# Attention with a gated feed-forward block on one core: a smaller first weight piece and short dummies at the start, the last block finished bank by bank at the end

## The chip, the core and the metric

The kernel runs on one core of a Trainium2 chip. The metric is the device time of one execution in microseconds (us). A profiled execution has a trace; its span is about 1.3 us shorter than the device time of the same execution (1284.5 against 1285.8).

Engines: TensorE (PE in the profile; its weight loads are PEld), VectorE (DVE), ScalarE (ACT), GpSimd (POOL), SyncE (SP, which here only issues transfers). PSUM is the memory, in banks, that TensorE's results land in. A dummy is a matmul whose result nobody reads; it stands at the start, where TensorE would otherwise be idle.

## The reference

```python
xn = layernorm(x)                                   # x: 2048 x 512
q  = (xn @ wq) in 32 heads of 128
o  = softmax(q k^T / sqrt(128)) v                   # k, v: 2048 cached rows a head
s  = o @ wo
h  = relu(xn @ W_gate) * (xn @ W_up)                # 512 -> 1792, 14 column blocks of 128
g  = silu(h @ W_down)
out = x + s * g
```

## The kernel before

It starts with the feed-forward block, one row block of 512 rows at a time, and the layernorm of the later row blocks is woven into the first one. The first row block ("the head") is not normalised before its matmuls: its four row tiles are only centred (the row scale is put in later), so that TensorE can start early. (Shortened.)

```python
FCS = [0, min(3, FC), min(8, FC), FC]        # weight pieces, in column blocks
load_x0(sp, 0); load_x0(act, 1)              # x row tiles 0 and 1
load_w(sp, Wg, 0); load_w(act, Wu, 0)        # first piece of both weights
load_x0(sp, 2); load_x0(act, 3)
load_w(sp, Wg, 1); load_w(sp, Wu, 1)
load_xq(1)                                   # x row tiles 4 to 7
load_w(sp, Wg, 2); load_w(sp, Wu, 2)
for Q in range(2, QB): load_xq(Q)            # x row tiles 8 to 11, 12 to 15
...
def head_ln():                               # after ten dummies of 512 columns
    ctok = {0: head_transpose(0, head_center(0))}
    warm_mm(2)                               # two more
    for n in range(4):
        ... head_tile(n, 0); head_transpose(n + 1); head_tile(n, 1); head_tile(n, 2)
```

Column blocks 0 to 2 of the head occupy the three slots of a ring of two PSUM banks each. Block 3 therefore waits for slot 0 (`ring_acquire`), until ScalarE's ReLU and VectorE's multiply of block 0 have read it. VectorE runs in program order, and between the multiplies of the first row block stand the layernorm statistics of later rows:

```python
def finish_gate_up(Q, fc, s, gtok, gu_tok):
    ... act.activation(gr_sb, gate bank, Relu)
    ... dve.tensor_tensor(hT[:, fc, :], gr_sb, up bank, mult)
    ring_tok[s] = [rtok, h_tok]
    if Q == 0: ln_task(fc)                   # statistics of row tile 4 + fc; every 4th: more
```

So the statistics of row tile 8 (`ln_task(4)`) come before the multiply of column block 5. At the end, the last attention block is normalised in two halves after all its score-times-value matmuls, then transposed on TensorE; then come the final output tiles 8 to 15 (output projection on TensorE; a multiply by g and an add of x on VectorE).

The softmax here doesn't subtract the row's maximum and nothing guards it: scores larger than these inputs give would overflow.

## Time and profile before

| | before |
|---|---|
| device time, median of 3 | 1286.27 us (1286.20 to 1286.35) |
| profiled execution | 1285.8 us, span 1284.5 us |
| busy share | TensorE 99%, ScalarE 78%, VectorE 30% |
| head's first gate tile | 6.32 us |
| second row block's first matmul | 44.02 us |
| last multiply of the output tiles | 1281.19 us |

The page of the profile says who is the bottleneck:

```profile
span 1284.5 us, 26708 instructions
...
PE 1266.6 (99%) x11813; PEld 835.2 (65%) x12040; DVE 380.5 (30%) x685; ACT 1001.7 (78%) x1109; POOL 13.2 (1%) x25
```

With TensorE at 99% only the two ends have room. The timeline of TensorE at the front (start, duration, engine, source line, operation, output and inputs, count; in brackets the idle time before and what ended it):

```profile
1.19 3.81 PE L369 MATMUL ps_r<-warm 128*128 128x512 bf16 x10 [1.19 <-DVE warm L234]
5.26 0.38 PE L359 MATMUL ps_acc<-ident,xc_sb 128*128 128x128 bf16 x4 [0.26 <-DVE xc_sb L349]
5.48 0.59 PE L369 MATMUL ps_r<-warm 128*128 128x512 bf16 x2
6.32 0.40 PE L397 MATMUL ps_r<-xcT,Wg_sb 128*128 128x128 bf16 x4 [0.24 <-ACT xcT L364]
...
13.15 0.81 PE L483 MATMUL ps_r<-xcT,Wg_sb 128*128 128x512 bf16 x3 [0.63 <-ACT gr_sb L449]
...
44.02 1.03 PE L483 MATMUL ps_r<-xnT,Wg_sb 128*128 128x512 bf16 x4
```

The line at 13.15 is block 3 waiting for its slot (one of its four matmuls is missing from the records; its first weight load is at 12.91):

```profile
12.91 0.56 PEld L483 LDWEIGHTS ps_r<-xcT,Wg_sb 128*128 128x128 bf16 x4 [0.56 <-ACT gr_sb L449]
```

The line at 44.02 is the first matmul of the second row block. From there to the end of the span it is 1240.5 us, so this start sums up everything that the front has won or lost.

VectorE at the end (L782 multiplies an output tile by g, L798 adds x, L688 and L691 normalise):

```profile
1271.02 0.69 DVE L782 TENSOR_TENSOR fin_tmp<-ps_r,g_sb 128x512 bf16<-128x512 f32 x1 [3.31 <-PE ps_r L774]
...
1273.59 0.17 DVE L688 RECIPROCAL rz_sb<-ps_acc 128x2 f32<-128x2 f32 x1 [0.60 <-PE ps_acc L737]
...
1274.33 0.42 DVE L691 TENSOR_TENSOR Onorm<-ps_acc,rz_sb 128x256 bf16<-128x256 f32 x1
1274.67 0.68 DVE L782 TENSOR_TENSOR fin_tmp<-ps_r,g_sb 128x512 bf16<-128x512 f32 x1
...
1275.60 0.68 DVE L782 TENSOR_TENSOR fin_tmp<-ps_r,g_sb 128x512 bf16<-128x512 f32 x1
...
1281.19 0.69 DVE L782 TENSOR_TENSOR fin_tmp<-ps_r,g_sb 128x512 bf16<-128x512 f32 x1
1281.79 0.75 DVE L798 TENSOR_TENSOR x_sb<-x_sb,fin_tmp 128x512 bf16<-128x512 bf16 x2
```

From 1274.67 on the multiplies follow each other every 0.93 us without idle time: VectorE, not TensorE, is the chain there.

### The profile page before, as it was taken

Reading aid. Unit: us, or ns where it says so; the run is one execution under the profiler, and the core shown is the slowest. Engines: PE = TensorE matmul, PEld = TensorE weight load, DVE = VectorE, ACT = ScalarE, POOL = GpSimd, SP = SyncE. Lnnn points to the kernel's source line nnn. Section 1 sums busy time; section 2 is a strip of 40 time slices with the busy share of each in tenths; the row PEclk is TensorE's granted clock in tenths of the full one; section 3 lists DMA queues with packets and bytes.
Section 4 is the critical chain, followed back from the end, with each engine's and each line's share of the span. In section 5 each row is a group of like instructions: output and inputs, shape, how many; then the busy total and the mean of one; then the engine's idle time right before and its main releaser. Section 6 shows DMA issues by size and latency. Waiting matters only on the chain.

```text
span 1284.5 us, 26708 instructions
## 1 busy us (share of the span) xinstructions
PE 1266.6 (99%) x11813; PEld 835.2 (65%) x12040; DVE 380.5 (30%) x685; ACT 1001.7 (78%) x1109; POOL 13.2 (1%) x25
## 2 busy tenths in 40 slices
PE   9999999999999999999999999999999999999998
PEld 5444466676666666666666666666666666666665
DVE  6433311112222222222222222222222222224355
ACT  3322399998888888888888888888888888888884
POOL 2100000000000000000000000000000000000000
PEclk9999999999999999999999999999999999999999
DMA  9600123232222332332221322323323322332202
GB/s 263 131 1 1 22 47 55 60 56 37 36 54 46 71 54 50 55 70 51 54 45 32 67 46 54 55 67 55 55 51 70 54 36 38 51 67 55 49 15 75
DMA packets 240977, 72.13 MB, mean 56 GB/s; under 512 B 227808, under 2 KB 240864, under 8 KB 240864
## 3 DMA queue, kind: packets, MB, share of 16 engines
q1 hardware_dynamic: 240048, 69.76, 28.5%
q8 instruction: 96, 1.57, 0.5%
q10 hardware_dynamic: 816, 0.66, 0.2%
q14 instruction: 17, 0.14, 0.0%
HBM read 32.77 MB, written 2.10 MB: 27 GB/s over the span
## 4 chain that ended last, share of the span: by engine, by line
PE 85%; ACT 12%; issue 1%; DVE 1%; DMA 0%; DVEq 0%
PE ps_acc L737 32%; PE ps_r L640 25%; ACT PT L650 12%; PE ps_r L573 9%; PE ps_r L594 8%; PE ps_acc L506 4%; PE ps_r L487 4%; PE ps_r L483 4%; PE ps_r L774 1%; DVE fin_tmp L782 0%; PE ps_r L397 0%; DMA x_sb<-in_A_x_dram 0%; DVE x_sb L798 0%; ACT gr_sb L449 0%; PE ps_acc L359 0%
## 5 line engine op out<-in xcount | busy, mean ns | idle before, releaser
L650 ACT ACTIVATE PT<-ps_r 128x1024 bf16<-128x1024 f32 x1024 | 952.5, 1054 | 167.7 <-PE ps_r L640 164.9
L737 PE MATMUL ps_acc<-V_sb,PT 128*128 128x129 bf16 x8192 | 776.5, 220 | 10.7
L737 PEld LDWEIGHTS ps_acc<-V_sb,PT 128*128 128x128 bf16 x8192 | 621.1, 98 | 241.7 <-ACT PT L650 3.5
L640 PE MATMUL ps_r<-QT_sb,KT_sb 128*128 128x512 bf16 x1837 | 675.1, 379 | 0.3
L667 DVE RECIPROCAL rz_sb<-ps_acc 128x4 f32<-128x4 f32 x127 | 23.3, 183 | 729.8 <-PE ps_acc L737 729.8
L640 PEld LDWEIGHTS ps_r<-QT_sb,KT_sb 128*128 128x128 bf16 x2048 | 195.0, 98 | 1.1 <-DVE QT_sb L584 0.4
L573 PE MATMUL ps_r<-xnT,Wq_sb 128*128 128x512 bf16 x511 | 130.9, 379 | 0.1
L594 PE MATMUL ps_r<-Wo_sb,OT_store 128*128 128x512 bf16 x447 | 114.4, 379 | 0.1
L584 DVE CAST QT_sb<-ps_r 128x512 bf16<-128x512 f32 x128 | 88.5, 692 | 48.1 <-PE ps_r L573 48.1
L573 PEld LDWEIGHTS ps_r<-xnT,Wq_sb 128*128 128x128 bf16 x512 | 49.9, 97 | 60.6 <-ACT PT L650 27.1
L670 DVE TENSOR_TENSOR Onorm<-ps_acc,rz_sb 128x512 bf16<-128x512 f32 x127 | 87.8, 691 | 4.4
L594 PEld LDWEIGHTS ps_r<-Wo_sb,OT_store 128*128 128x128 bf16 x448 | 43.8, 98 | 52.9 <-ACT PT L650 0.2
L449 ACT ACTIVATE gr_sb<-ps_r 128x512 bf16<-128x512 f32 x56 | 32.9, 595 | 49.6 <-PE ps_r L483 49.1
L607 DVE TENSOR_TENSOR s_acc<-s_acc,ps_r 128x512 f32<-128x512 f32 x96 | 66.0, 687 | 17.4 <-PE ps_r L594 17.4
L455 DVE TENSOR_TENSOR hT<-gr_sb,ps_r 128x512 bf16<-128x512 bf16 x56 | 38.4, 685 | 46.8 <-PE ps_r L487 42.2
L506 PE MATMUL ps_acc<-Wd_sb,hT 128*128 128x512 bf16 x220 | 48.8, 379 | 0.2
L487 PE MATMUL ps_r<-xnT,Wu_sb 128*128 128x512 bf16 x164 | 42.7, 379 | 0.2
L483 PE MATMUL ps_r<-xnT,Wg_sb 128*128 128x512 bf16 x165 | 42.6, 379 | 0.2
L506 PEld LDWEIGHTS ps_acc<-Wd_sb,hT 128*128 128x128 bf16 x224 | 21.9, 98 | 26.4
L514 ACT ACTIVATE sig_sb<-ps_acc 128x512 f32<-128x512 f32 x12 | 7.2, 597 | 29.5 <-PE ps_acc L506 29.5
L487 PEld LDWEIGHTS ps_r<-xnT,Wu_sb 128*128 128x128 bf16 x168 | 16.4, 98 | 19.8
L483 PEld LDWEIGHTS ps_r<-xnT,Wg_sb 128*128 128x128 bf16 x168 | 16.4, 98 | 19.8
(50 smaller groups left out, 181.0 us busy)
## 6 DMA issues: line engine op xcount, KB each, us to landing
V_sb<-in_A_v_cache_dram SPq DMA_DIRECT2D x32, 512.0 KB, 4.8
Wq_sb<-in_A_wq_dram SPq DMA_DIRECT2D x32, 128.0 KB, 2.5
Wo_sb<-in_A_wo_dram SPq DMA_DIRECT2D x8, 512.0 KB, 4.9
OT_store<-Onorm SPq DMA_TRANSPOSE x127, 2.4
Wd_sb<-in_B_W_down_dram SPq DMA_DIRECT2D x1, 1792.0 KB, 14.6
x_sb<-in_A_x_dram SPq DMA_DIRECT2D x3, 512.0 KB, 12.1
out_dram<-x_sb SPq DMA_DIRECT2D x6, 256.0 KB, 2.2
Wg_sb<-in_B_W_gate_dram SPq DMA_DIRECT2D x1, 768.0 KB, 10.3
```

Of the source, the lines that this page charges most:

```text
L455: dve.tensor_tensor(hT[par][:, fc, :], gr_sb[gk][:], ps_r[:, gb + 1, :], ALU.mult)
L483: ins = pe.matmul(ps_r[:, gb, :], Wg_sb[:, c, fs], xT[:, c, xs], start=(c == 0), stop=(c == DC - 1))
L487: ins = pe.matmul(ps_r[:, gb + 1, :], Wu_sb[:, c, fs], xT[:, c, xs], start=(c == 0), stop=(c == DC - 1))
L506: ins = pe.matmul(ps_acc[:, jb, 0:D], hT[par][:, fc, j * 128:(j + 1) * 128], Wd_sb[:, fc, :], start=(fc == 0), stop=(fc == FC - 1))
L573: ins = pe.matmul(ps_r[:, bank, :], Wq_sb[b][:, c, :], xnT[:, c, qs], start=(c == 0), stop=(c == DC - 1))
L584: etok = sem_qpe.sig(dve.tensor_copy(QT_sb[b][:, qs], ps_r[:, bank, :]))
L594: ins = pe.matmul(ps_r[:, bank, 0:D], OT_store[g % 2][:, hh, n * 128:(n + 1) * 128], Wo_sb[g % 2][:, hh, :], start=(hh == 0), stop=(hh == ...
L607: dve.tensor_tensor(s_acc[:, n, :], s_acc[:, n, :], ps_r[:, bank, 0:D], ALU.add)
L640: ins = pe.matmul(ps_r[:, 2 * s + tt, :], KT_sb[h % 2][:, t * 128:(t + 1) * 128], QT_sb[h % 2][:, qs], start=True, stop=True)
L650: act.activation(PT[pb][:], ps_r[:, 2 * s:2 * s + 2, :], ACTF.Exp, scale=scale)
L670: dve.tensor_tensor(Onorm[ob][:], o_ap, rz_sb[:].to_broadcast([128, 4, Dh]), ALU.mult))
L737: ins = pe.matmul(o_ap, PT[pb][:, tt, j * 128:(j + 1) * 128], V_sb[vb][:, t, 0:VW], start=(t == 0 and j % 2 == 0), stop=(t == KT - 1 and j ...
```

## The change

Its intent at the front: the first weight piece is smaller, so that it lands sooner; the dummies, which are meant to bring TensorE's clock up, are shorter and need no tile cleared by VectorE; block 3 uses the two accumulator banks, which are idle then. At the end: tiles 8 and 9 go ahead of the last score-times-value matmuls, these are done bank by bank, and ScalarE normalises the first bank. The core of the diff (shortened; lines left out are not marked one by one):

```diff
-        FCS = [0, min(3, FC), min(8, FC), FC]
+        FCS = [0, 2, 5, 9, FC]
-        warm_w = sem_ln1.sig(dve.memset(warm[:], 0.0))
-        load_x0(act, 3)
+        load_x0(sp, 3)
         load_w(sp, Wg_sb, wg_src, sem_wg, 2)
         load_w(sp, Wu_sb, wu_src, sem_wu, 2)
+        load_w(sp, Wg_sb, wg_src, sem_wg, 3)
+        load_w(sp, Wu_sb, wu_src, sem_wu, 3)
         for Q in range(2, QB):
             load_xq(Q)
@@ dummies: 18 and 4 of 256 columns in place of 10 and 2 of 512
-                pe.matmul(ps_r[:, 2 * NSLOT - 1, 0:D], warm[:, 0:128], warm[:], ...)
+                pe.matmul(ps_r[:, 2 * NSLOT - 1, 0:256], ones_w, ones_r, ...)
@@ head_ln: another order of tiles and transposes, blocks 0 and 1 first (cut)
@@ emit_gate_up
-                s = ring_acquire()
+                if Q == 0 and fc == HFC:
+                    s = None                     # the two accumulator banks
+                    _wait_all(pe, acc_free)
+                else:
+                    s = ring_acquire()
@@ emit_norm_last
+            if bank == 0:
+                for j in range(2):
+                    act.activation(Onorm[ob][:, j, :], o_ap[:, j, :], ACTF.Copy, scale=rz_sb[:, j, 0:1])
@@ end
+        emit_M([(emit_final_tile, NT - 8), (emit_final_tile, NT - 7)])
+        for bank in range(2):
+            for gq in range(TOTP - LAG, TOTP):
+                for tt in range(2):
+                    emit_PV_tile(gq, tt, (bank,))
+        emit_M([(emit_final_tile, NT - 6)])
+        flush_last_transposes()
+        emit_M([(emit_final_tile, NT - 5)])
```

More of the change, by code (lines that the diff above doesn't have):

```diff
@@ L133, in bass_recurrent_scan__mha_block_cached__glu_gated_reglu__prompt_kernel @@
         PT = [S_([128, 2, NQ], BF16, "PT") for _ in range(NPB)]
-        warm = S_([128, D], BF16, "warm")
         es_b = ExitStack()
@@ L159, in bass_recurrent_scan__mha_block_cached__glu_gated_reglu__prompt_kernel @@
         sem_x0 = [newsem(16) for _ in range(4)]
-        sem_wg = [newsem(16) for _ in range(3)]
-        sem_wu = [newsem(16) for _ in range(3)]
+        sem_wg = [newsem(16) for _ in range(4)]
+        sem_wu = [newsem(16) for _ in range(4)]
         sem_xq = [newsem(16) for _ in range(QB)]
@@ L239, in bass_recurrent_scan__mha_block_cached__glu_gated_reglu__prompt_kernel @@
         load_x0(sp, 2)
-        load_x0(act, 3)
+        load_x0(sp, 3)
         load_w(sp, Wg_sb, wg_src, sem_wg, 1)
         load_w(sp, Wu_sb, wu_src, sem_wu, 1)
-        if QB > 1:
-            load_xq(1)
+        load_xq(1)
         load_w(sp, Wg_sb, wg_src, sem_wg, 2)
         load_w(sp, Wu_sb, wu_src, sem_wu, 2)
+        load_w(sp, Wg_sb, wg_src, sem_wg, 3)
+        load_w(sp, Wu_sb, wu_src, sem_wu, 3)
         for Q in range(2, QB):
@@ L365, in head_transpose @@
             return acc_free[n % 2]
+        ones_w = nc.const_aps.tensor(1.0, [128, 128], BF16)
+        ones_r = nc.const_aps.tensor(1.0, [128, 256], BF16)
         def warm_mm(k):
             for _i in range(k):
-                pe.matmul(ps_r[:, 2 * NSLOT - 1, 0:D], warm[:, 0:128], warm[:], start=True, stop=True)
+                pe.matmul(ps_r[:, 2 * NSLOT - 1, 0:256], ones_w, ones_r, start=True, stop=True)
         def head_ln():
-            ctok = {0: head_transpose(0, head_center(0))}
-            warm_mm(2)
-            for n in range(4):
-                if n + 1 < 4:
-                    ntok = head_center(n + 1)
-                _wait(pe, ctok[n])
-                head_tile(n, 0)
-                if n + 1 < 4:
-                    ctok[n + 1] = head_transpose(n + 1, ntok)
-                for fc in range(1, HFC):
-                    head_tile(n, fc)
+            c0 = head_transpose(0, head_center(0))
+            warm_mm(4)
+            c1 = head_transpose(1, head_center(1))
+            n2 = head_center(2)
+            n3 = head_center(3)
+            _wait(pe, c0)
+            head_tile(0, 0)
+            head_tile(0, 1)
+            _wait(pe, c1)
+            head_tile(1, 0)
+            head_tile(1, 1)
+            c2 = head_transpose(2, n2)
+            head_tile(0, 2)
+            head_tile(1, 2)
+            _wait(pe, c2)
+            head_tile(2, 0)
+            c3 = head_transpose(3, n3)
+            head_tile(2, 1)
+            head_tile(2, 2)
+            _wait(pe, c3)
+            for fc in range(HFC):
+                head_tile(3, fc)
         half_slots = []
@@ L392, in head_tile @@
             for i, (W, sems) in enumerate(((Wg_sb, sem_wg), (Wu_sb, sem_wu))):
-                if n == 0 and fc == 0:
-                    pe.wait_ge(sems[0].h, 16)
+                if n == 0 and fc in FCS:
+                    pe.wait_ge(sems[FCS.index(fc)].h, 16)
                 ins = None
@@ L441, in bass_recurrent_scan__mha_block_cached__glu_gated_reglu__prompt_kernel, with gu_banks @@
         hT_free = [None, None]
+        def gu_banks(s):
+            if s is None:
+                return ps_acc[:, 0, :], ps_acc[:, 1, :]
+            return ps_r[:, 2 * s, :], ps_r[:, 2 * s + 1, :]
         def finish_gate_up(Q, fc, s, gtok, gu_tok):
             par = Q % 2
-            gb = 2 * s
+            g_ps, u_ps = gu_banks(s)
             gk = fc % NSLOT
@@ L448, in finish_gate_up @@
             _wait(act, gr_free[gk])
-            rtok = sem_relu.sig(act.activation(gr_sb[gk][:], ps_r[:, gb, :], ACTF.Relu))
+            rtok = sem_relu.sig(act.activation(gr_sb[gk][:], g_ps, ACTF.Relu))
             _wait(dve, gu_tok)
@@ L454, in finish_gate_up @@
             h_tok = sem_h.sig(
-                dve.tensor_tensor(hT[par][:, fc, :], gr_sb[gk][:], ps_r[:, gb + 1, :], ALU.mult)
+                dve.tensor_tensor(hT[par][:, fc, :], gr_sb[gk][:], u_ps, ALU.mult)
             )
             gr_free[gk] = h_tok
-            ring_tok[s] = [rtok, h_tok]
+            if s is None:
+                y_bank_free[:] = [h_tok, h_tok]
+            else:
+                ring_tok[s] = [rtok, h_tok]
             if Q == 0:
@@ L471, in emit_gate_up @@
                     continue
-                s = ring_acquire()
-                gb = 2 * s
+                if Q == 0 and fc == HFC:
+                    s = None
+                    _wait_all(pe, acc_free)
+                else:
+                    s = ring_acquire()
+                g_ps, u_ps = gu_banks(s)
                 if fc == 0:
@@ L482, in emit_gate_up @@
                 for c in range(DC):
-                    ins = pe.matmul(ps_r[:, gb, :], Wg_sb[:, c, fs], xT[:, c, xs],
+                    ins = pe.matmul(g_ps, Wg_sb[:, c, fs], xT[:, c, xs],
                                     start=(c == 0), stop=(c == DC - 1))
@@ L486, in emit_gate_up @@
                 for c in range(DC):
-                    ins = pe.matmul(ps_r[:, gb + 1, :], Wu_sb[:, c, fs], xT[:, c, xs],
+                    ins = pe.matmul(u_ps, Wu_sb[:, c, fs], xT[:, c, xs],
                                     start=(c == 0), stop=(c == DC - 1))
@@ L533, in bass_recurrent_scan__mha_block_cached__glu_gated_reglu__prompt_kernel @@
         assert DC == 4 and QB >= 2 and FC >= 4 * (QB - 1) + 2
-        _wait(pe, warm_w)
-        warm_mm(10)
+        warm_mm(18)
         head_ln()
@@ L688, in emit_norm_last @@
             rtok = sem_rz.sig(dve.reciprocal(rz_sb[:, js, :], z_ap[:, js, :]))
+            if bank == 0:
+                _wait(act, rtok)
+                for j in range(2):
+                    tok = sem_otc.sig(
+                        act.activation(Onorm[ob][:, j, :], o_ap[:, j, :], ACTF.Copy,
+                                       scale=rz_sb[:, j, 0:1]))
+                emit_last_transposes(hh, Q, ob, bank, tok)
+                return tok
             _wait(dve, rtok)
@@ L718, in bass_recurrent_scan__mha_block_cached__glu_gated_reglu__prompt_kernel, with emit_PV_tile @@
         pending_last = []
-        def emit_PV_tile(gp, tt):
+        def emit_PV_tile(gp, tt, banks=(0, 1)):
             b, h, Q, p = blk_of(gp)
@@ L731, in emit_PV_tile @@
             t = 2 * p + tt
-            for j in range(4):
+            for j in range(2 * banks[0], 2 * banks[-1] + 2):
                 bank = j // 2
@@ L738, in emit_PV_tile @@
                                 start=(t == 0 and j % 2 == 0), stop=(t == KT - 1 and j % 2 == 1))
-                if b == NBLK - 1 and t == KT - 1 and j == 1:
-                    tx = sem_pv.sig(ins)
-                if t == KT - 1 and j == 3:
+                if t == KT - 1 and j % 2 == 1 and (j == 3 or b == NBLK - 1):
                     ty = sem_pv.sig(ins)
             if t == KT - 1:
+                if b == NBLK - 1:
+                    emit_norm_last(b, banks[0], ty)
+                    return
                 if Q == QB - 1 and h + 2 < H:
@@ L746, in emit_PV_tile @@
                     issue_v(h + 2)
-                if b < NBLK - 1:
-                    ntok = emit_norm_block(b, ty)
-                    norm_tok[b] = (ntok, ntok)
-                else:
-                    emit_norm_last(b, 0, tx)
-                    emit_norm_last(b, 1, ty)
+                ntok = emit_norm_block(b, ty)
+                norm_tok[b] = (ntok, ntok)
         def sp_head_start(h):
@@ L832, in bass_recurrent_scan__mha_block_cached__glu_gated_reglu__prompt_kernel @@
         glu_done_tok = sem_g.cur()
-        for step in range(LAG, TOTP + LAG):
-            gp = step
-            gq = step - LAG
+        for gp in range(LAG, TOTP):
+            gq = gp - LAG
             bq, hq, Qq, pq = blk_of(gq)
             items = plan.pop((bq, pq), None)
-            if gp < TOTP:
-                b, h, Q, p = blk_of(gp)
-                if p == 0 and Q == 0:
-                    sp_head_start(h)
-                open_S_pair(gp)
-                emit_S_tile(gp, 0)
-                if items:
-                    emit_S_tile(gp, 1)
+            b, h, Q, p = blk_of(gp)
+            if p == 0 and Q == 0:
+                sp_head_start(h)
+            open_S_pair(gp)
+            emit_S_tile(gp, 0)
             if items:
+                emit_S_tile(gp, 1)
                 emit_M(items)
             emit_PV_tile(gq, 0)
-            if gp < TOTP and not items:
+            if not items:
                 emit_S_tile(gp, 1)
@@ L854, in bass_recurrent_scan__mha_block_cached__glu_gated_reglu__prompt_kernel @@
         assert not plan
-        for n in range(NT - 8, NT - 4, 2):
-            emit_M([(emit_final_tile, n), (emit_final_tile, n + 1)])
-            if n == NT - 8:
-                flush_last_transposes()
+        emit_M([(emit_final_tile, NT - 8), (emit_final_tile, NT - 7)])
[6 more added lines that the diff above has]
+        emit_M([(emit_final_tile, NT - 5)])
         for n in range(NT - 4, NT, 2):
```

## The prediction

> **What bounds the kernel.** TensorE. The page gives it 99% of a 1284.5 us span; ScalarE has 78%, VectorE 30%. The change touches only the first 13 us and the last 13 us, so at most a few microseconds of 1286.27 are in reach. I read both ends from the timeline.
>
> **Front, before.** The first x tile lands and VectorE starts at 3.81 us; the first transpose is at 5.26, the first gate tile at 6.32 (released by ScalarE's copy of xcT, not by the weights, which land 4.9 us after an issue at 1.20, so at 6.1). From there the three transposes (0.22 us each) and twelve 8-matmul tiles (0.44 us each) run without a gap; the last weight load of them ends at 12.35. Then column block 3 waits for a ring slot: its first weight load is at 12.91, the waits view puts 0.6 us to this. The slot needs block 0's ReLU and VectorE multiply (12.15 to 12.84).
>
> **Front, after.**
> - Block 3 uses the two accumulator banks, free since the fourth xcT copy (about 10.9). The 0.57 us wait goes; block 4 needs slot 0 at about 14.1, which is free at 12.84. From there to the end of the first feed-forward block TensorE is unbroken in the trace, so this is a shift of everything behind. Gain 0.57 us.
> - The smaller first weight piece helps no wait that this trace shows. Estimate from the landings (1.31 MB by 6.88 us, then 0.36 MB/us): piece 0 at 5.4, third x tile at 5.8 instead of 6.9, piece 1 at 7.3 (gate) and 8.3 (up). Block 2 first needs piece 1 at about 8.6 and 8.8: it fits, by less than 0.5 us.
> - Transposing tile 1 before the first gate tile costs 0.22 us of start but is only moved work: the end of the head stays at 12.35.
> - Short dummies cover the same time (18 of 256 columns against 10 of 512). They can start about 0.3 us sooner, without VectorE's memset. The Trainium skill, "TensorE: Matmul & The Clock Gate", Part 1, says the activity window that releases the clock is free-running and 3.4 us long; the trace shows the full clock from about 4.5 us. I expect it there again, before the first transpose: gain 0.
>
> **Tail, before.** VectorE's chain: TensorE finishes the last block at 1273.56, normalisation takes 1.08 us, then eight multiply/add pairs at a pitch of 0.93 us, from 1274.67 to 1282.54. TensorE's tile takes 0.86.
>
> **Tail, after (estimate from the same durations).** Tiles 8 and 9 run before the last three score pairs: their multiplies at 1273.2 and 1274.1. Bank 0's reciprocal at 1275.06, ScalarE scales bank 0; bank 1's reciprocal waits for TensorE until 1275.44, its multiply ends at 1276.06. But tile 10 comes from TensorE only after the 24 matmuls, so its multiply is at 1276.30, tile 11's, behind the transposes, at 1277.40; then 0.93 each: tile 15 at 1281.12 against 1281.19. VectorE's idle time is moved, not removed: gain 0.07 us.
>
> Sum 0.64 us: predicted 1285.63 us, 8 times in 10 within 1284.9 to 1286.25. Faster by over 2%: 0.005; within 2%: 0.99; slower: 0.005.
>
> **What would show it.** No wait before block 3's first weight load, at about 12.35; no wait for weights in the head; tile 10's multiply waiting for TensorE; the last multiply near 1280.5 (0.57+0.07 sooner); attention unchanged in length.
>
> **What would make it wrong.** Piece 1 landing after 8.6 us stalls the head by the difference. ScalarE's two scalings slower than 0.8 us would delay the transposes. A clock released one window later would cost over a microsecond. In the tail 0.2 us either way, since VectorE and TensorE are nearly level there.

## More of the kernel before

Most of this study is about differences of a few tenths of a microsecond in 1286, so single executions, medians and windows of the trace are kept apart throughout.

## The result

| | before | changed |
|---|---|---|
| device time, median of 6 | 1286.21 us (1285.95 to 1286.35) | 1285.66 us (1285.53 to 1285.98) |
| profiled span | 1284.5 us | 1284.4 us |

The ratio is 0.9996 with a 95% interval of 0.9983 to 1.0009. A ratio here is the mean time of one kernel's runs over that of the other's of the same rounds, so it is not quite the ratio of the medians quoted. The interval is wider than the whole effect. The medians differ by 0.55 us and the two ranges of six runs nearly part, while 0.64 us had been predicted: as a number the prediction was right. Yet the two profiled spans differ by only 0.1 us, and the front does not look as predicted. TensorE in the changed kernel:

```profile
0.77 4.00 PE L371 MATMUL ps_r<-const-bfloat16-1.0 128*128 128x256 bf16 x18 [0.77 <-PEq L906]
4.93 0.38 PE L358 MATMUL ps_acc<-ident,xc_sb 128*128 128x128 bf16 x4 [0.16 <-DVE xc_sb L348]
...
6.28 0.39 PE L410 MATMUL ps_r<-xcT,Wg_sb 128*128 128x128 bf16 x4
...
12.18 1.03 PE L508 MATMUL ps_acc<-xcT,Wg_sb 128*128 128x512 bf16 x4
...
21.34 1.02 PE L508 MATMUL ps_r<-xcT,Wg_sb 128*128 128x512 bf16 x4 [0.37 <-DVE hT L473]
...
44.03 1.03 PE L508 MATMUL ps_r<-xnT,Wg_sb 128*128 128x512 bf16 x4
```

Block 3 indeed no longer waits: it starts at 12.18, and its first weight load is 0.79 us ahead of before:

```profile
12.12 0.59 PEld L508 LDWEIGHTS ps_acc<-xcT,Wg_sb 128*128 128x128 bf16 x4
```

Of the 0.79 us, 0.56 are the wait; the other 0.23 are the head's own, which ended at 12.12 where the prediction kept 12.35. But block 8 waits at 21.34, which is new, and the second row block starts at 44.03, where it started before. The lead was given back: 0.53 us of it at block 8 (block 7 starts at 19.08 against 19.84 before, block 9 at 23.07 against 23.30), and the rest at the third tile of the first down projection, where the weight loads wait 0.56 us for VectorE's `g_sb`. The chain of waits (start, duration, what) leaves TensorE at 20.12 and comes back to it only at that tile, at 37.97:

```profile
19.25 0.88 PE ps_r L508 x4
20.12 0.02 issue
20.15 0.60 ACT gr_sb L467
...
21.11 0.69 DVE stats L313
21.80 0.59 DVE hT L473
...
37.97 6.22 PE ps_acc L531 x28
```

and VectorE's timeline shows what it had waited for:

```profile
18.16 0.69 DVE L473 TENSOR_TENSOR hT<-gr_sb,ps_r 128x512 bf16<-128x512 bf16 x1 [0.92 <-ACT gr_sb L467]
19.62 0.69 DVE L313 BATCH_NORM_STATS2 stats<-x_sb 128x6 f32<-128x512 bf16 x1 [0.78 <-DMA x_sb<-in_A_x_dram]
...
20.51 0.69 DVE L473 TENSOR_TENSOR hT<-gr_sb,ps_r 128x512 bf16<-128x512 bf16 x1
```

The line at 19.62 is the statistics of row tile 8, waiting 0.78 us for the transfer of x. Behind it, in program order, stands the multiply of block 5 (20.51), which frees the slot that block 8 needs. In the kernel before, the same statistics waited 0.19 us:

```profile
19.22 0.69 DVE L314 BATCH_NORM_STATS2 stats<-x_sb 128x6 f32<-128x512 bf16 x1 [0.19 <-DMA x_sb<-in_A_x_dram]
```

The end went as predicted, term by term:

```profile
1271.04 0.69 DVE L811 TENSOR_TENSOR fin_tmp<-ps_r,g_sb 128x512 bf16<-128x512 f32 x1 [3.31 <-PE ps_r L803]
...
1276.30 0.69 DVE L811 TENSOR_TENSOR fin_tmp<-ps_r,g_sb 128x512 bf16<-128x512 f32 x1 [0.23 <-PE ps_r L803]
...
1277.39 0.69 DVE L811 TENSOR_TENSOR fin_tmp<-ps_r,g_sb 128x512 bf16<-128x512 f32 x1
...
1281.13 0.69 DVE L811 TENSOR_TENSOR fin_tmp<-ps_r,g_sb 128x512 bf16<-128x512 f32 x1
```

Tile 10's multiply is at 1276.30, tile 11's at 1277.39, the last at 1281.13: within 0.01 us of the estimate, but on the clock of a front that has won nothing, so that the prediction's own test, a last multiply near 1280.5, failed. From the first line shown to the last it is 10.09 us against 10.17 before.

So two questions were open. Where does the lead go, and why are the medians 0.55 us apart when two profiles are not?

### The profile page after: what moved, and what is told of

It is laid out like the page before. It is cut to its first block, busy times and chain, and to the rows that moved or that the text cites. A ratio compares the mean times of both kernels' runs of the same rounds, so it can differ in the third digit from the quotient of the medians. Undisturbed runs are those within 1.5% of the kernel's fastest.

```text
span 1284.4 us, 26956 instructions
## 1 busy us (share of the span) xinstructions
PE 1279.1 (100%) x12050; PEld 836.4 (65%) x12050; DVE 380.5 (30%) x683; ACT 1002.2 (78%) x1111; POOL 13.2 (1%) x25
## 4 chain that ended last, share of the span: by engine, by line
PE 98%; DVE 1%; ACT 0%; issue 0%; DMA 0%; ACTq 0%; DVEq 0%
PE ps_acc L769 36%; PE ps_r L664 34%; PE ps_r L597 9%; PE ps_r L618 8%; PE ps_acc L531 3%; PE ps_r L508 3%; PE ps_r L512 3%; PE ps_r L803 1%; DVE stats L313 0%; PE ps_r L410 0%; DVE hT L473 0%; DMA x_sb<-in_A_x_dram 0%; DVE fin_tmp L811 0%; ACT gr_sb L467 0%; DVE x_sb L827 0%
## 5 line engine op out<-in xcount | busy, mean ns | idle before, releaser
L664 PE MATMUL ps_r<-QT_sb,KT_sb 128*128 128x512 bf16 x2048 | 754.1, 379 | 0.0
```

What stands on the lines that cost most here:

```text
L664: ins = pe.matmul(ps_r[:, 2 * s + tt, :], KT_sb[h % 2][:, t * 128:(t + 1) * 128], QT_sb[h % 2][:, qs], start=True, stop=True)
```

## The experiments

Twelve kernels ran, four at a time on one chip, each in five rounds beside the kernel before. That kernel's own median was 1286.21, 1286.16 and 1286.22 us in the three jobs, so the medians below may be set side by side. No ratio's interval excludes 1; what is told apart is told by the medians with their ranges and by the windows.

| run | median us (range) | ratio | second row block starts, profiled run |
|---|---|---|---|
| null_before | 1286.21 (1285.64 to 1286.31) | 0.9999 | 44.43 |
| tail_only | 1286.11 (1285.84 to 1286.31) | 0.9999 | 44.43 |
| front_only | 1285.76 (1285.46 to 1286.10) | 0.9997 | 44.33 |
| before_short_dummies | 1286.10 (1285.85 to 1286.57) | 1.0001 | 44.31 |
| before_acc3 | 1285.71 (1285.31 to 1286.06) | 0.9997 | 43.92 |
| after_again | 1285.71 (1285.47 to 1285.80) | 0.9994 | 44.00 |
| x2_early | 1285.02 (1284.92 to 1285.83) | 0.9993 | 43.30 |
| after_old_pieces | 1285.20 (1284.87 to 1285.72) | 0.9993 | 43.43 |
| old_pieces_long_dummies | 1285.61 (1285.39 to 1286.21) | 0.9994 | 43.94 |
| x2_pool_add | 1285.88 (1285.81 to 1286.13) | 0.9999 | 43.58 |
| old_pieces_pool3 | 1285.11 (1284.81 to 1286.16) | 0.9991 | 44.62 |
| old_pieces_x2_pool3 | 1284.93 (1284.64 to 1285.63) | 0.9990 | 43.26 |

### Nulls: null_before and after_again

The unchanged kernels, with new profiles.

> The kernel before, unchanged, as a null. Its first profile was of a run of 1285.8 us, 0.4 below its median of 1286.2, and started x's first tile at 3.81 us against 3.48 in the changed kernel. Theory A (start-up scatter): the ratio to the kernel before is 1.000, and this profile's span, or its first x landing, differs from the first profile by some tenths of a microsecond though nothing was changed. Theory B (the first landing is earlier because of the change): x's first tile lands at 3.8 us again, within 0.05.

```profile
1.19 4.45 PE L369 MATMUL ps_r<-warm 128*128 128x512 bf16 x10 [1.19 <-DVE warm L234]
5.43 0.63 PE L359 MATMUL ps_acc<-ident,xc_sb 128*128 128x128 bf16 x4
5.85 0.99 PE L369 MATMUL ps_r<-warm 128*128 128x512 bf16 x2
6.74 0.40 PE L397 MATMUL ps_r<-xcT,Wg_sb 128*128 128x128 bf16 x4
```

This is TensorE's timeline of the kernel before, in a more typical execution (1286.24 us). Theory A held: with nothing changed, x's first tile landed at 3.33 us instead of 3.81, and still the front was slower by 0.42 us. The full clock came later: the ten dummies took 4.45 us instead of 3.81, all of them at the slow rate (one starts every 0.43 us; at the full clock it is every 0.22), and TensorE was still busy with them when the first centred tile was ready (4.63), so the first transpose had to wait until 5.43; the two further dummies then held the first gate tile until 6.74. The first profile, on which the prediction rested, was one in which the clock came early, 0.47 us below the median of its three. That answers the second question: the two first profiles compare one of the quickest executions of before with a middling one of the changed kernel.

In the trace's own record of the clock, the full rate came at 4.22 us in the first profile of before and at 6.64 in the null, at 4.77 in the first profile of the changed kernel, and between 4.1 and 7.0 us over the thirteen of the fourteen profiles that have the record. The Trainium skill, "TensorE: Matmul & The Clock Gate", Part 1, says of this that the activity window is free-running and that the number of slow matmuls at the start varies from run to run. These runs agree as to the variation (4.22 and 6.64 us with one and the same kernel); none shows the window itself.

> The changed kernel as it is, a null for the changed side on the same chip as the next three. 1285.5 to 1286.0 us, median near 1285.7; the second block row starts at 43.9 to 44.4 us, with TensorE waiting at column block 8 whatever the clock did.

1285.71 us and 44.00 us came as expected. The wait came elsewhere: not at block 8 but in the head, 0.7 us of the weight loads at block 2 for the second piece of the up weights (0.5 between the matmuls). The lead was lost before VectorE could take it.

### front_only and tail_only

The two halves of the diff, each on the other half of the kernel before.

> The changed front with the old tail. Theory (front leads and is given back): block 3 starts at about 12.1 us without a wait, 0.8 sooner than in the first profile of before, but column block 8 waits 0.5 us or so at 21 and the first down projection 0.2 at 38, so the second block row starts at 44.0 as before; last multiply at about 1281.2, time 0.1 to 0.5 us below before. Rival (the front's gain is kept and the tail is what is worth nothing): second block row starts near 43.3, time 0.6 below before or more.

> The old front with the changed tail. From the last score matmul's group to the end of the last add I expect 0.06 us less than before (predicted 0.07, first profile of after: 0.08 from the start of final tile 6 to the last multiply). Time 0 to 0.15 us below before: not to be told from 0 by the clock on the wall, only by the windows. A rival in which the tail made the 0.55 us that the medians show expects 0.5 us below before.

The front alone gave 1285.76 us, 0.45 below before, and its profile has the same waits as the changed kernel: 0.9 us of VectorE for row tile 8, 0.5 us of TensorE for VectorE's multiply, and 0.3 us of the weight loads in the head for the up weights. Its second row block starts at 44.33 rather than the 44.0 that I had written. The tail alone gave 0.10 us by the medians and 10.09 us against 10.17 from the first to the last multiply: 0.08 us, where 0.07 had been predicted. The rival, that the tail made the 0.55 us, is out.

### x2_early: does the transfer of x take the lead back?

```diff
         load_w(sp, Wu_sb, wu_src, sem_wu, 2)
+        load_xq(2)
         load_w(sp, Wg_sb, wg_src, sem_wg, 3)
         load_w(sp, Wu_sb, wu_src, sem_wu, 3)
-        for Q in range(2, QB):
-            load_xq(Q)
+        load_xq(3)
```

> The changed kernel with x's third row block (tiles 8 to 11) loaded ahead of the last weight piece instead of behind it. Theory D (the front's lead is given back because VectorE, in order, waits 0.8 us for x tile 8, which lands at 19.6, before the multiply that frees column block 8's slot): no wait for x at 18.8, no wait at column block 8, none or under 0.1 at the third tile of the first down projection; second block row starts at 43.2 to 43.4 instead of 44.03, and the time falls by 0.6 to 0.8 us to about 1285.0. Rival C (the lead is given back by the in-order chain VectorE, square root and ReLU on ScalarE, whatever x does): the wait moves but the second block row still starts at 43.9 to 44.05 and the time stays at 1285.6. The last weight piece comes about 1.5 us later (about 19), needed at about 22.5: no wait expected.

```profile
18.81 0.69 DVE L313 BATCH_NORM_STATS2 stats<-x_sb 128x6 f32<-128x512 bf16 x1
```

The statistics of row tile 8 start at 18.81 without a wait, block 8 does not wait, the second row block starts at 43.30 us and the median falls to 1285.02 us. Theory D is shown: the lead was taken by VectorE's wait for x, through program order. The rival C is out; its chain through ScalarE still has its 0.92 us waits, but they cost TensorE nothing here.

### before_short_dummies and before_acc3: single parts on the kernel before

The first is only the exchange of dummies, the second only block 3 in the accumulator banks, as in the diff above.

> The kernel before with only the change's dummies: 18 and 4 of 256 columns on a constant, in place of 10 and 2 of 512 on a cleared tile. In the null run the full clock came at about 6.7 us (4.4 in the first profile), the ten long dummies then held TensorE until 5.43 though the first centred tile was ready at 4.65, and the two that follow held the first gate tile until 6.74. Theory F (the dummies' length is what the change gains in runs with a late clock): first transpose follows the centred tile within 0.3 us whatever the clock, first gate tile at 6.3 or sooner, time 0.3 to 0.5 us below before (about 1285.8). My prediction's theory (the dummies are worth nothing) expects 1286.2 and the first gate tile at 6.3 to 6.7 as before.

> The kernel before with only column block 3 moved to the accumulator banks. The prediction's term: block 3's wait of 0.56 us goes and the whole rest moves up by 0.57, time about 1285.65. Theory D (the lead is given back to VectorE's wait for x tile 8): block 3 starts 0.5 us or more sooner after the last head tile, with no wait, but a wait at VectorE for x tile 8 grows and a wait of TensorE appears at column block 7 or 8, or at the third down tile, so the second block row starts at 44.0 to 44.2 and the time falls by 0.1 to 0.4 only.

Short dummies alone gained 0.06 us: my theory F failed as it stood. The first transpose did come at 4.88 us with a late clock, but in the profiled execution the first gate tile then met the weights, which landed at about 6.6:

```profile
4.88 0.58 PE L357 MATMUL ps_acc<-ident,xc_sb 128*128 128x128 bf16 x4
5.26 1.06 PE L370 MATMUL ps_r<-const-bfloat16-1.0 128*128 128x256 bf16 x4
6.63 0.38 PE L398 MATMUL ps_r<-xcT,Wg_sb 128*128 128x128 bf16 x4 [0.32 <-DMA Wg_sb<-in_B_W_gate_dram]
```

That holds for this execution. In the nine profiles with the old first piece its gate half landed anywhere between 5.4 and 7.0 us, so why all five executions together gained only 0.06 stays open.

Block 3 alone gained 0.45 us by the medians, and its second row block starts 0.51 us before that of the null. The lead was kept, which theory D as I had written it did not expect: x tile 8 had landed before VectorE wanted it (19.43, no wait). Two things differ from the changed kernel. By the trace's landing records x came sooner, at 19.00 against 19.60, so something in the changed kernel made x late. And this execution had a late clock (5.9 us) and the long dummies, so VectorE also came 0.59 us later than in the changed kernel, where it was ready at 18.84.

### after_old_pieces: the weight pieces

```diff
-        FCS = [0, 2, 5, 9, FC]
+        FCS = [0, 3, 8, FC]
-        load_w(sp, Wg_sb, wg_src, sem_wg, 3)
-        load_w(sp, Wu_sb, wu_src, sem_wu, 3)
```

> The changed kernel with the old three weight pieces (3, 5 and 6 column blocks). The first piece then is 768 KB of both weights and lands near 6.1 us in the first profile of before; the changed front wants its first gate tile at about 6.2 us, so I expect a wait for weights of 0 to 0.3 us in the head, the third x tile's landing near 6.8, and, because the lead is given back later anyway, a time within 0.15 us of the changed kernel's 1285.66. If the small first piece is worth something of its own, the time is 0.3 us or more above that.

1285.20 us: undoing this part of the change makes it 0.46 us faster, beyond the 0.15 that I had allowed. The expected wait for weights in the head came (0.2 us of the weight loads). VectorE reaches row tile 8 at 18.93 and does not wait, though with little to spare, since x had landed at 18.89:

```profile
18.93 0.69 DVE L311 BATCH_NORM_STATS2 stats<-x_sb 128x6 f32<-128x512 bf16 x1
```

The chain of waits stays on TensorE from block 3 to the second row block:

```profile
12.51 0.86 PE ps_acc L506 x4
13.37 0.86 PE ps_acc L510 x4
14.24 0.86 PE ps_r L506 x4
...
31.50 12.09 PE ps_acc L529 x56
43.59 0.86 PE ps_r L506 x4
```

The reason lies in the transfers. The windows view of 4 to 19 us has the stretch, its length, the busy time of TensorE, its weight loads, VectorE, ScalarE and GpSimd with their instructions, the granted clock, the mean busy share of the DMA engines and, last, the GB/s that they moved. First the kernel before, then the changed kernel, then this run:

```profile
4.00:19.00 15.00, 13.87 (x146) 9.41 (x146) 10.45 (x25) 5.78 (x11) 0.00 (x0) 1.00 1.08 360
```

```profile
4.00:19.00 15.00, 14.55 (x152) 9.89 (x151) 10.06 (x25) 6.24 (x12) 0.00 (x0) 1.00 1.09 348
```

```profile
4.00:19.00 15.00, 14.69 (x151) 10.08 (x150) 10.14 (x26) 6.07 (x12) 0.00 (x0) 1.00 1.08 360
```

The engines are full in all three, but with the smaller pieces they move 348 GB/s instead of 360. The other profiles agree: 359 to 361 in all nine with the old pieces, 348 to 350 in all five with the new ones. A piece of two column blocks is cut into runs of 512 bytes a row, one of six into 1536. By the trace's records of single packets in the first 20 us, a packet of 512 bytes takes 27.8 ns on average, one of 768 bytes 40.4 and one of 1280 bytes 59.4 (all three in the changed kernel), and one of 1536 bytes 69.7 (before): 18.4 bytes a nanosecond for the shortest and 22.0 for the longest. Over 15 us, 12 GB/s are 0.18 MB, which at 0.36 MB/us makes everything behind about 0.5 us late, and what stands behind is x's third row block. The landing records bear this out: behind the old pieces it landed at 18.76 to 19.19 us in eight profiles, behind the new ones at 19.57 to 19.91 in three. So it is shown that the new pieces make x late, and that undoing them, or loading x ahead of the last of them, removes the wait. That the length of the runs is the reason is argued from the packets' times, not tried by itself. The 32 more four-byte packets of the changed kernel, of 10 ns each over 16 engines, come to 0.02 us and are not the reason.

The old pieces have their own risk, and the profile of old_pieces_pool3 shows it: there the first piece landed late and TensorE waited 0.81 and 0.44 us between matmuls for it (execution of 1286.16 us, the other four of that kernel at 1284.81 to 1285.12). This is what the small first piece guards against. But its guard moves the wait to the second piece: 0.3 us of the weight loads in the profile of front_only, 0.7 in those of after_again and x2_pool_add (0.2 and 0.5 between the matmuls).

### old_pieces_long_dummies: the dummies again, where the lead counts

> The changed kernel with the old three pieces and also the old dummies (10 and 2 of 512 columns on a tile that VectorE clears). Alone on the kernel before, the short dummies gained 0.06 us, because the weights then landed no sooner than 6.6 us. Theory F2 (with the wait behind the head gone, TensorE's lead in the head counts, and long dummies take some of it away when the clock comes late): 0.2 to 0.4 us above the old pieces with short dummies (1285.2), so about 1285.5; the first transpose starts at 5.4 instead of 4.9 in a run with a late clock. If the dummies are worth nothing: 1285.2.

With the lead no longer thrown away, the old dummies cost 0.41 us by the medians (1285.61 against 1285.20, on two chips): the late-clock profile has its first transpose at 5.43 and its first gate tile at 7.05, where after_old_pieces has 4.94 and 6.29. Theory F2 held in the main; these medians too have ranges that overlap.

### x2_pool_add, old_pieces_pool3, old_pieces_x2_pool3: a version that beats both

At the end VectorE's 0.93 us a tile is above TensorE's 0.86, so adds were moved to GpSimd: five of them (tiles 10 to 14), then every second one (10, 12, 14). The core of the second version's diff:

```diff
-            ftok = sem_opa.sig(
-                dve.tensor_tensor(x_sb[:, n, :], x_sb[:, n, :], fin_tmp[fb][:], ALU.add))
+            if n in (NT - 6, NT - 4, NT - 2):
+                eng, sem = pool, sem_padd
+                _wait(pool, base_done[n])
+            else:
+                eng, sem = dve, sem_opa
+            _wait(eng, mtok)
+            ftok = sem.sig(
+                eng.tensor_tensor(x_sb[:, n, :], x_sb[:, n, :], fin_tmp[fb][:], ALU.add))
```

> The kernel with x's third row block loaded early, and the adds of the final tiles 10 to 14 on GpSimd instead of VectorE, for a version that beats both. VectorE's pitch for a final tile falls from 0.93 us to 0.6, so TensorE's 0.86 sets the pace: last multiply 0.3 us sooner, and tile 14's add leaves the end of the chain, 0.3 more. Expected 0.4 to 0.6 us below the 1285.02 of the early load, about 1284.5; if GpSimd's add takes over 1.5 us[...], nothing or a loss.

> For a version that beats both: the changed kernel with the old three pieces and the adds of final tiles 10, 12 and 14 on GpSimd (1.18 us each, measured with five of them, which queued up there), the others on VectorE. TensorE's 0.86 us a tile then sets the pace, the last multiply comes 0.25 to 0.3 us sooner behind the start of the tail and tile 14's add is off the end: 0.4 to 0.6 us below the old pieces, about 1284.7.

> The same, and x's third row block loaded ahead of the last (third) weight piece. With the old pieces VectorE did not wait for x tile 8 (it began at 18.93 without a wait), so theory D expects nothing: within 0.15 us of the run before this one. A gain of 0.3 or more would mean that x still limits there.

Five adds on GpSimd were a miss, 1285.88 us. The timeline:

```profile
1276.62 5.92 POOL L834 TENSOR_TENSOR x_sb<-x_sb,fin_tmp 128x512 bf16<-128x512 bf16 x5 [1237.84 <-DVE fin_tmp L812]
...
1281.12 0.43 DVE L834 TENSOR_TENSOR x_sb<-x_sb,fin_tmp 128x512 bf16<-128x512 bf16 x1
```

One add takes 1.18 us there, longer than a tile's 0.86, so they queue and the last ends at 1282.54, 1.0 us after VectorE's. From the second row block to the end of the span it is 1241.2 us, against 1240.4 with the adds on VectorE. With three of them the last multiply does come sooner, but only by 0.21 us: 9.88 us from the multiply of tile 6 to that of tile 15 (1270.27 to 1280.15) against 10.09. From tile 6's multiply to the end of the last add it is 11.26 us against 11.44. The last add took 0.66 us there, others 0.41 to 0.43; why is open. So 0.2 us, not the 0.4 to 0.6 expected; by the medians 1285.11 against 1285.20 with the old pieces. The early load on top gave 1284.93, 0.18 us lower than without, where within 0.15 was expected; with ranges of 1.0 us and more over five executions each, I do not call that difference shown.

The best version is thus the changed kernel with the three old weight pieces, x's third row block loaded ahead of the last piece, and three adds on GpSimd: 1284.93 us against 1285.71 for the changed kernel and 1286.22 for the kernel before, on the same chip. That is 0.1%, and the interval of its ratio (0.9976 to 1.0003) still holds 1.

## Why the prediction was right, and where it was not

The number, 1285.63 us against 1285.66 measured, is right, but by luck: its largest term was lost, and terms that it had put at nothing made up for it. Point by point:

- **"The 0.57 us wait goes" and "this is a shift of everything behind".** The wait went. Alone on the kernel before it is worth 0.45 us. In the changed kernel the shift failed: the first profile of the changed kernel is 0.79 us ahead at block 3 and level at the second row block. I had checked that TensorE is unbroken from there in the trace of before, but not how much slack those stages have in the other engines. The sign was in the timeline to be read: VectorE already waited 0.19 us for row tile 8, so in an execution with an early clock anything that moved TensorE and VectorE forward would meet that transfer, even had it not come later.
- **"The smaller first weight piece helps no wait that this trace shows", block 2 "fits, by less than 0.5 us".** The estimate of landings took a constant 0.36 MB/us. With shorter runs it was 348 GB/s instead of 360. Block 2's up weights landed at 8.54 us in the first profile (8.3 estimated) and just fitted; they came late in three of the five profiles of kernels with the new pieces, by 0.3 to 0.7 us of the weight loads, and x's third row block came late. Measured by undoing it, this part costs 0.46 us in the changed kernel (by the medians; the ranges, 1284.87 to 1285.72 and 1285.53 to 1285.98, overlap a little). The prediction had named the first risk; it had missed the second.
- **Clock "there again", dummies' "gain 0".** The first profile had the clock early; the null had it late. I knew from the skill that the window is free-running and still took one execution's phase for the kernel's. The risk was also mis-sized: the clock of the null came 2.4 us later and its second row block started 0.41 us later, not over a microsecond. The short dummies and the earlier start are worth 0.41 us beside the old weight pieces, and nearly nothing (0.06) alone.
- **Tail, "gain 0.07 us".** 0.08 in the windows, with each step within 0.03 us of the estimate.

The sum as measured by the medians, taking each part where it was tried: block 3, minus 0.45; dummies, minus 0.41; weight pieces, plus 0.46; tail, minus 0.10. That is minus 0.50 us against the 0.55 seen (1286.21 to 1285.66). The parts were not all tried on the same base, and the new order of the head's tiles was not tried alone, so this is a check of size and not a proof. So the prediction's two errors, a cost that it missed (the pieces) and a gain that it denied (the dummies), nearly cancelled.

## What to carry to other kernels

Before counting a removed wait as a shift of everything behind it, look at which transfers and which in-order engines stand level with the bottleneck a few microseconds later: here a wait of 0.2 us for a transfer, in one profile, was the sign that a lead of 0.8 us would not last. Cutting a load into smaller pieces can lower the rate of the whole queue (here 348 against 360 GB/s, with the shorter runs as the likely reason), and what it delays may be a tensor that is not being cut. And where a start-up phase varies from execution to execution, take a second profile before costing tenths of a microsecond from the first.

## What the Trainium skill lacked or had wrong

- "DMA: Bandwidth & Descriptors", Specifications, gives 512 bytes and up as enough for line rate. Here 512-byte packets moved 18.4 bytes a nanosecond and DMA engine, 1536-byte ones 22.0, and the whole load ran at 348 against 360 GB/s, so that row did not quite hold here. "Perfetto Trace Analysis", DMA Optimizations, which puts significant overhead on transfers under 2 KB, fits these runs better if it is read of the packets into which a transfer is cut.
- "TensorE: Matmul & The Clock Gate", Part 1, says in one place that the transition varies by 500 ns, in another that the number of slow matmuls is run-variable. Here the full clock came anywhere from 4.1 to 7.0 us after the span's start, and at 4.22 and 6.64 us in two executions of one kernel; the first figure is too small.
- "GPSIMD Engine Reference" times an add only for longer rows of fp32, and no page that I found gives the time of a GpSimd add of two 128x512 bf16 operands: 1.18 us here, against 0.42 on VectorE.
